# Attention scores and row maxima in four 32-row tiles of TensorE in place of two 64-row tiles

## The chip, the cores and the metric

The kernel runs on one core of a Trainium2 chip. The metric is the device time of one execution in microseconds (us), the median of several runs. The engines are named as in the profile: PE is TensorE (matmuls; PEld is its weight load, which overlaps them), DVE is VectorE, ACT is ScalarE, POOL is GpSimd and SP is the sync engine, which issues the DMAs (SPq is its queue). Matmul results go to PSUM, here used as eight banks of 128 partitions x 512 fp32 numbers. "L246" is line 246 of the kernel before.

## The reference

One transformer block without biases, on 2048 tokens of width 448, in fp32: layer norm, multi-query attention (16 heads of 28 dimensions that share one key and one value head, softmax over all 2048 keys, output projection, residual), then layer norm and a gated feed-forward of width 1792 with a residual.

```python
q = (ln(x) @ wq) in 16 heads of 28;  k = ln(x) @ wk;  v = ln(x) @ wv
p = softmax(q k^T * 28 ** -0.5);     h = x + concat(p v) @ wo
out = h + (silu(ln(h) @ w1) * (ln(h) @ w3)) @ w2
```

## The kernel before

**Numbers in two parts.** Matmuls in the format fp32r keep fewer bits than fp32, so most operands are split into a rounded part and a rest, both fp32r, and a product is the sum of rounded x rounded, rest x rounded and rounded x rest. For a wide product these are separate matmuls that add up in one PSUM bank (`mm_D`, L121, line 128 in the profile). The product of weights and values (`pv`, L296, line 300) is in plain fp32; the profile shows two matmul instructions for each of its calls.

**Scores.** Scores are made transposed: 128 keys on the partitions, 512 queries along the row. A head has 28 dimensions, so with four spare rows it takes 32 partitions; the four heads of a group stand below each other in the projection's output. In the kernel before, a score matmul is 64 rows deep: `KS` holds the rounded keys on rows 0-31 and their rests on rows 32-63 (and a copy of both on rows 64-127), and the queries of one head are laid out twice, on both halves of the same 64 rows. So two matmuls per head (`Head.mm`, L282, line 287), with the rounded queries and with their rests, make all four partial products. Head `j` of a group uses rows 0-63 if `j` is even and 64-127 if it is odd. `build_qs` (L206) splits the queries into `qst` (ACT and POOL) and lays them out by eight DMAs (line 223) in `QS`.

**Row maxima.** Softmax needs each query's largest score before the exponential. It is found ahead by separate matmuls, the units (`Unit`, L228, line 241): rounded queries as the weights, so 128 queries stand on the partitions and 512 keys along the row, and one VectorE `tensor_reduce` (line 246) takes the maximum into `MX`. When all 64 units of a block are done, `max_done` (L256) reduces and splits the maxima into `NEG`, `max_rows` (L265) transposes it on VectorE, and `max_out` (L270) puts it by four DMAs (line 274) into spare rows of `QS`, which meet ones in `KS`. So the score matmul itself subtracts the maximum, and `Head.exp` (L289, line 293) is one ScalarE exponential from a bank to `pt`.

**The loop.** A block `i` is 512 queries and four heads (16 blocks), a step is one block with 128 keys (16 per block, 256 steps). In each of the first 236 steps (L626) TensorE does the four heads' scores of step `s`, four units of step `s + AHEAD` (20 steps on), and `pv` of step `s - 1`. The order in a step is written out by hand and differs between even and odd steps: `pair` makes two heads beside each other, `beside` a head and units. What happens at certain steps only (building queries, maxima, dividing by the softmax sum in `o_norm` and `o_mul`, splitting weights, `wo_rows`) is filed by step with `at` and called by `run`. The last 20 steps (L670) have no units left. A start stage (L382 to L564) does layer norm and the projections `kv` and `q` with the first 80 units between them (`first`, `pairs`); a feed-forward stage follows the loop.

**Banks.** Seven banks serve everything but `po`, the sum of `pv`, which has the eighth. `bank` takes the one longest in the free list and `done` appends it; both act when the program is written, so the assignment is fixed, and on the chip a matmul into a bank waits for the bank's last reader. The program order of each engine is the order in which the code names the operations.

Of the kernel before, what the change touches and what calls it, by code (L numbers as in the profile page):

```python
# [35 lines left out]
def block_kernel(  # L36
# [25 lines left out]
    qs_pool = ctx.enter_context(tc.tile_pool(name="qs", bufs=3))  # L62
# [9 lines left out]
    KS = keep.tile([P, S], F32R, name="KS", tag="ks")  # L72
# [20 lines left out]
    def put_w2_ks():  # L93
        tl = keep.tile([P, S], F32, name="w2_ks", tag="ks")
        for k in range(4):
            W2[4 + k] = tl[:, T * k : T * k + D]
# [9 lines left out]
    free, used = list(range(7)), {}  # L106

    def bank(name="pb"):
# [97 lines left out]
    def build_qs(i, ps=None):  # L206
        t, g = divmod(i, NG)
        st = wk_pool.tile([P, 2, T], F32R, name="qst")
        if ps is None:
            q = QR[t][:, g]  # L210
            se.activation(st[:, 0], q, AF.Copy)  # L211
            ge.tensor_tensor(st[:, 1], q, f(st[:, 0]), op=ALU.subtract)  # L212
        else:
            se.activation(st[:, 0], ps, AF.Copy)
            ve.tensor_tensor(st[:, 1], ps, f(st[:, 0]), op=ALU.subtract)
# [12 lines left out]
    class Unit:  # L228

        def __init__(self, i, p, n, kt, jj):
            self.i, self.p, self.n, self.kt, self.jj = i, p, n, kt, jj

        def mm(self):
            i, n, kt, r = self.i, self.n, self.kt, rows(self.jj)
# [3 lines left out]
            pe.matmul(self.ps, QS[i][r, self.p, n * P : (n + 1) * P], KS[r, kt * T : (kt + 1) * T],  # L241
                      start=True, stop=True)

        def red(self):
            c = 8 * self.jj + 4 * self.p + self.n
            ve.tensor_reduce(MX[self.i][:, c, self.kt : self.kt + 1], self.ps, axis=AX.X, op=ALU.max)  # L246
            done(self.ps)

    def both(i, p, n, kt):
        us = [Unit(i, p, n, kt, jj) for jj in range(2)]  # L250
        for u in us:
            u.mm()
        for u in us:
            u.red()

    def max_done(i):  # L256

        nm, neg = wk_pool.tile([P, 16], F32, name="nm"), NEG[i % 2]
        ve.tensor_reduce(nm, MX[i], axis=AX.X, op=ALU.max, negate=True)
        hi, lo = [neg.rearrange("q (j k c) -> q j k c", j=2, k=2)[:, :, k] for k in range(2)]  # L260
        n2 = nm.rearrange("q (j c) -> q j c", j=2)
        ge.tensor_copy(hi, n2)
        ge.tensor_tensor(lo, n2, f(hi), op=ALU.subtract)
# [6 lines left out]
    def max_out(i):  # L270
        mr = f(MR.pop(i))
        to = f(QS[i][28::32, :2]).rearrange("m p (n a q) -> m (p n) a q", n=NQ, a=4)
        for a in range(4):
            sy.dma_start(to[:, :, a], mr[32 * a : 32 * a + 32])

    class Head:
# [5 lines left out]
        def mm(self, k):  # L282
            i, c, (p, jj) = self.i, self.c, divmod(self.j, 2)
            if k == 0:
                self.ps = bank()
            r = rows(jj)
            pe.matmul(self.ps, KS[r, c * P : (c + 1) * P], QS[i][r, 2 * k + p], start=(k == 0), stop=(k == 1))  # L287

        def exp(self):  # L289
            i, c, (p, jj) = self.i, self.c, divmod(self.j, 2)  # L290
            if (i, c, p) not in PT:
                PT[i, c, p] = pt_tile()
            se.activation(f(PT[i, c, p][:, jj]), self.ps, AF.Exp, bias=0.0, scale=SCALE)  # L293
            done(self.ps)

    def pv(i, c):  # L296
        if c == 0:
            PO[i] = ps_o.tile([P, T], F32, name="po")
        for j in range(4):
            pe.matmul(PO[i][32 * j : 32 * j + 32], VA[:, c], f(PT[i, c, j // 2][:, j % 2]),  # L300
                      start=(c == 0), stop=(c == NC - 1))
        if c == NC - 1:
            g = i % NG
            if i < NI - 2:
                se.activation(OT[:, g], PO.pop(i), AF.Copy)
# [48 lines left out]
    def split_w(k):  # L354
        ws = qs_pool.tile([P, 4, T], F32R, name="qs")
        wh, wl = [ws[:, 2 * b : 2 * b + 2].rearrange("p a (c m e) -> p (a c) m e", c=2, m=2) for b in range(2)]
        ve.tensor_copy(wh, W13[k])
        ge.tensor_tensor(wl, W13[k], f(wh), op=ALU.subtract)  # L358
        return wh, wl

    def split_w2(k):
        w2s = wk_pool.tile([P, 2, T], F32R, name="qst")
# [3 lines left out]

    def a_units(step):

        i, c = divmod(step, NC)
        if i >= NI:  # L370
            return None
        p, n = divmod(c // 2, NQ)
        us = [Unit(i, p, n, 2 * (c % 2) + k, jj) for jj in (1, 0) for k in range(2)]
        return us if step % 2 == 0 else [us[0], us[2], us[3], us[1]]

# [6 lines left out]
    with tc.tile_pool(name="start", bufs=1) as sp:  # L382
        wq_r = wo_r = OT[:, :, :D]
        WQ = [w.rearrange("p c (h r) -> p c h r", h=H) for w in OS]
        wkv_r = sp.tile([P, 4, 96], F32, name="wkv_r")
        WKV = [sp.tile([P, 4, 96], F32R, name=f"WKV{k}") for k in range(2)]
        ones = sp.tile([P, 1], F32, name="ones")
        ve.memset(wkv_r, 0.0)
        se.activation(ones, ident[:, 60:61], AF.Identity, bias=ident[:, 28:29], scale=-1.0)
# [3 lines left out]
        for m0, w in ((0, wk), (64, wv)):  # L393
# [5 lines left out]
        def copy_wk():  # L399
            ve.tensor_copy(wkv_r[:, :, 32 : 32 + DH], wkv_r[:, :, :DH])  # L400
# [32 lines left out]
        def kv(t, nb=0):  # L433
            cols = slice(t * T, (t + 1) * T)
            ps = bank()
            mm_D(ps[:96], WKV, XT[t], slice(0, 96), slice(0, T), lambda: pairs(nb))

            se.activation(KS[0:64, cols], ps[0:64], AF.Identity, bias=ones[0:64], scale=1.0)
            ve.tensor_tensor(KS[32:64, cols], ps[32:64], f(KS[32:64, cols]), op=ALU.subtract)
            vt = sp.tile([P, T], F32, name="vt", bufs=2)  # L440
            se.activation(vt[64:96], ps[64:96], AF.Copy)
            sy.dma_start(f(KS[64:128, cols]), f(KS[0:64, cols]))
# [3 lines left out]
        def va(t, vt):  # L446
            ps = bank()
            for n in range(NQ):
                pe.transpose(ps[:, 32 * n : 32 * n + 32], vt[64:96, n * P : (n + 1) * P], ident[64:96, 64:96])  # L449
# [14 lines left out]
        first = [(both, 0, *divmod(pn, NQ), kt) for kt in range(4) for pn in range(8)]  # L464
        first.append((max_done, 0))
        for c in range(AHEAD - NC):
            first += [(both, 1, *divmod(c // 2, NQ), 2 * (c % 2) + k) for k in range(2)]
# [150 lines left out]
    def pair(a, b):  # L618
        for k in range(2):
            a.mm(k)  # L620
            b.mm(k)
        a.exp()
        b.exp()

    prev, tail = None, False
    for s in range(LAST - AHEAD):  # L626
        i, c = divmod(s, NC)
        au = a_units(s + AHEAD)
        hs = [Head(i, c, j) for j in range(4)]

        def beside(h, us):
            for k in range(2):
                h.mm(k)
                us[k].mm()
            h.exp()

        def red(us):
            for u in us:
                u.red()

        pair(hs[0], hs[1])
        if c % 2 == 0:
            beside(hs[2], au[:2])
            run(s + 0.4)
            red(au[:2])
            run(s + 0.5)
            if prev is not None:
                pv(*prev)
            run(s + 0.7)
            beside(hs[3], au[2:])  # L650
            red(au[2:])
        else:
            pair(hs[3], hs[2])
            for u in au[:2]:
                u.mm()
            run(s + 0.4)
            red(au[:2])
            run(s + 0.5)
            pv(*prev)
            run(s + 0.7)  # L660
            for u in au[2:]:
                u.mm()
            red(au[2:])
        prev = (i, c)
        run(s)
# [3 lines left out]
    TAIL = LAST - AHEAD  # L669
    for s in range(TAIL, LAST):  # L670
        i, c = divmod(s, NC)
# [4 lines left out]
        hs = [Head(i, c, j) for j in range(4)]  # L676
        for k in range(2):
            hs[0].mm(k)
            hs[1].mm(k)
        if s == TAIL:  # L680
            pv(*prev)
# [3 lines left out]
        hs[0].exp()  # L685
        hs[1].exp()
        pair(hs[2], hs[3])
# [127 lines left out]
```

## Time and profile before

| | |
|---|---|
| median of 3 runs | 1219.92 us (1219.85 to 1220.7) |
| profiled execution, first to last instruction (its own time, in the span) | 1218.0 us |
| granted TensorE clock, mean | 1.000 |
| DMA traffic of the span | 47.34 MB, mean 39 GB/s |
| first and last exponential of the attention loop's heads | at 90 and 774 us |
| first and last reduce of a unit | at 31 and 735 us |

The page's first table gives each engine's busy time and its share of the span. A group's row reads: line, engine, operation, output<-inputs, shapes, count, then busy time, mean ns of one, idle time of the engine just before, and what ended most of it. A row of the timeline reads: start, length, engine, line, operation, count. A row of the windows reads: stretch, its length, busy time (count) of PE, PEld, DVE, ACT and POOL, granted clock, DMA share, GB/s.

### The profile page before, as it was taken

The numbers are of one execution on the slowest core, as the hardware profiler recorded it, in microseconds if no ns is written. First come the engines' busy times: TensorE is split into PE (matmuls) and PEld (weight loads), VectorE is DVE, ScalarE is ACT, GpSimd is POOL, SyncE is SP. The second block draws the span as 40 slices with busy tenths as digits, with TensorE's granted clock in tenths as the row PEclk, the third lists the DMA queues.
The fourth block names the chain that finished last, engine by engine and source line by source line (L and its number), as shares of the span: only waits on it lengthen the run. The fifth ranks groups of instructions, "written<-read, shape, count | busy, mean of one in ns | idle before, by whom it ended". The sixth has DMA issues, their size and how long they took to land.

```text
span 1218.0 us, 19886 instructions
## 1 busy us (share of the span) xinstructions
PE 1204.7 (99%) x7564; PEld 760.6 (62%) x7564; DVE 858.8 (71%) x1476; ACT 663.4 (54%) x1251; POOL 332.0 (27%) x281
## 2 busy tenths in 40 slices
PE   6999999999999999999999999999999999999998
PEld 5764444446444445444446444688888888888887
DVE  7999999998999998999998992164343334333333
ACT  4427887885888885888786789512111111111111
POOL 4320001101001110110122012254555555555552
PEclk9999999999999999999999999999999999999999
DMA  6120111211210221221121100133000000000000
GB/s 205 33 70 1 46 39 46 52 44 50 52 43 12 53 51 42 53 47 35 26 57 42 47 18 19 49 85 110 1 31 1 1 1 31 1 1 31 1 1 31
DMA packets 46526, 47.34 MB, mean 39 GB/s; under 512 B 14944, under 2 KB 33120, under 8 KB 46432
## 3 DMA queue, kind: packets, MB, share of 16 engines
q1 hardware_dynamic: 46432, 46.09, 14.4%
q8 instruction: 59, 0.97, 0.3%
q14 instruction: 35, 0.29, 0.1%
HBM read 20.37 MB, written 3.80 MB: 20 GB/s over the span
## 4 chain that ended last, share of the span: by engine, by line
PE 98%; DVE 1%; DMA 0%; SPq 0%; ACT 0%; issue 0%; POOL 0%; DVEq 0%
PE pa L128 27%; PE pb L287 26%; PE po L300 21%; PE pb L722 11%; PE pa L241 8%; PE pb L128 4%; PE pb L190 1%; DMA wkv_r<-in_A_wk_dram 0%; DVE st L156 0%; DVE xn L174 0%; DVE X L726 0%; SPq L378 0%; DVE mx L246 0%; DVE OS L411 0%; PE pb L449 0%
## 5 line engine op out<-in xcount | busy, mean ns | idle before, releaser
L246 DVE TENSOR_REDUCE mx<-pa 128x1 f32<-128x512 f32 x1024 | 637.0, 683 | 26.0 <-PE pa L241 3.1
L293 ACT ACTIVATE pt<-pb 128x512 f32<-128x512 f32 x996 | 517.8, 602 | 125.1 <-PE pb L287 96.2
L287 PE MATMUL pb<-qs,KS 64*128 64x512 f32 x2048 | 348.6, 399 | 0.0
L287 PEld LDWEIGHTS pb<-qs,KS 64*128 64x128 f32 x2048 | 227.7, 184 | 142.2 <-DVE mx L246 95.9
L241 PE MATMUL pa<-KS,qs 64*128 64x512 f32 x1024 | 283.2, 437 | 0.1
L300 PE MATMUL po<-pt,VA 128*32 128x512 f32 x1992 | 265.0, 604 | 0.0
L128 PE MATMUL pa<-xh,qs 128*128 128x512 f32 x896 | 235.2, 395 | 0.0
L241 PEld LDWEIGHTS pa<-KS,qs 64*128 64x128 f32 x1024 | 129.1, 184 | 129.6 <-DVE mx L246 103.2
L128 PEld LDWEIGHTS pa<-xh,qs 128*128 128x128 f32 x896 | 168.6, 188 | 37.8 <-issue 0.8
L710 DVE TENSOR_TENSOR pt<-pa,pt 128x512 f32<-128x512 f32 x56 | 38.7, 691 | 205.7 <-PE pa L128 205.7
L722 PE MATMUL pb<-qst,pt 128*128 128x448 f32 x672 | 147.8, 368 | 0.0
L708 ACT ACTIVATE pt<-pa 128x512 f32<-128x512 f32 x56 | 33.5, 599 | 193.9 <-PE pa L128 193.7
L722 PEld LDWEIGHTS pb<-qst,pt 128*128 128x128 f32 x672 | 125.2, 188 | 13.6 <-DVE pt L714 0.3
L713 ACT ACTIVATE pt<-pt 128x512 fp32r<-128x512 f32 x56 | 35.4, 633 | 157.5 <-DVE pt L710 157.5
L128 PE MATMUL pa<-xl,qs 128*128 128x512 f32 x336 | 96.3, 395 | 0.0
L300 PEld LDWEIGHTS po<-pt,VA 128*32 128x32 f32 x1992 | 40.1, 108 | 78.8 <-issue 74.5
L358 POOL TENSOR_TENSOR qs<-QR,qs 128x1024 fp32r<-128x1024 f32 x32 | 76.8, 2400 | 25.6 <-PE pa L128 16.2
L128 PEld LDWEIGHTS pa<-xl,qs 128*128 128x128 f32 x336 | 63.3, 188 | 14.6
L714 DVE TENSOR_TENSOR pt<-pt 128x512 fp32r<-128x512 f32 x56 | 44.7, 798 | 39.1 <-ACT pt L713 39.1
L329 POOL TENSOR_TENSOR OT<-OT,rb 128x512 f32<-128x512 f32 x15 | 19.3, 1289 | 190.6 <-DMA rb<-sd 166.0
L364 POOL TENSOR_TENSOR qst<-w_wo,qst 128x448 fp32r<-128x448 f32 x24 | 35.8, 1490 | 94.2 <-DVE qst L363 94.2
L212 POOL TENSOR_TENSOR qst<-QR,qst 128x512 fp32r<-128x512 f32 x15 | 19.3, 1285 | 145.4 <-ACT qst L211 145.4
(90 smaller groups left out, 656.7 us busy)
## 6 DMA issues: line engine op xcount, KB each, us to landing
qs<-qst SPq DMA_DIRECT2D x128, 128.0 KB
rb<-sd SPq DMA_DIRECT2D x64, 64.0 KB
QR<-OT SPq DMA_DIRECT2D x60, 56.0 KB
QR<-in_B_w_dram SPq DMA_DIRECT2D x16, 192.0 KB
X<-in_A_x_dram SPq DMA_DIRECT2D x3, 896.0 KB
out_dram<-X SPq DMA_DIRECT2D x3, 896.0 KB
w<-in_B_w_dram SPq DMA_DIRECT2D x8, 192.0 KB
w_wo<-in_B_w_dram SPq DMA_DIRECT2D x6, 224.0 KB
```

Source lines behind the costliest of these rows:

```text
L128: pe.matmul(ps, lhs[b][:, cb, lsl], rhs[a][:, ca, rsl], start=(k == 0), stop=(k == len(terms) - 1),)
L241: pe.matmul(self.ps, QS[i][r, self.p, n * P : (n + 1) * P], KS[r, kt * T : (kt + 1) * T], start=True, stop=True)
L246: ve.tensor_reduce(MX[self.i][:, c, self.kt : self.kt + 1], self.ps, axis=AX.X, op=ALU.max)
L287: pe.matmul(self.ps, KS[r, c * P : (c + 1) * P], QS[i][r, 2 * k + p], start=(k == 0), stop=(k == 1))
L293: se.activation(f(PT[i, c, p][:, jj]), self.ps, AF.Exp, bias=0.0, scale=SCALE)
L300: pe.matmul(PO[i][32 * j : 32 * j + 32], VA[:, c], f(PT[i, c, j // 2][:, j % 2]), start=(c == 0), stop=(c == NC - 1))
L358: ge.tensor_tensor(wl, W13[k], f(wh), op=ALU.subtract)
L364: ge.tensor_tensor(w2s[:, 1, :D], W2[k], f(w2s[:, 0, :D]), op=ALU.subtract)
L710: ve.tensor_tensor(sg, ps[1], sg, op=ALU.mult)
L713: se.activation(h[:, 0], sg, AF.Copy)
L714: ve.tensor_tensor(h[:, 1], sg, f(h[:, 0]), op=ALU.subtract)
L722: pe.matmul(Y[t][n][:, :D], hid[a][:, n * P : (n + 1) * P], w2s[:, b, :D], start=(k == 0 and m == 0), stop=(k == NF - 1 and m == 2))
```

## The change

A head's scores are made in a row tile of its own, 32 rows deep, four tiles side by side. The rounded keys (`KS[0]`) and their rests (`KS[1]`) become two tiles, each with four copies below each other, and the queries stay as the projection leaves them, four heads below each other, rounded part and rest in `QS[i][:, 0]` and `[:, 1]`. A head now takes three matmuls (rounded x rounded, key rest x rounded query, rounded key x query rest), and a unit uses one row tile. The eight DMAs of `build_qs` go; `max_out` issues eight DMAs of 16 rows instead of four of 32, for rounded maxima and rests separately (spare rows 28 and 29 of each tile). The order within two steps is the list `EVERY`: `h0` is the next of three matmuls for heads 0 and 1, `h1` for heads 2 and 3, `u3` a unit in row tile 3, and `pv` the product with the values; what is filed for a step is called around `pv`. `bank` picks the free bank that is due first by a running count, to which `on_pe` adds matmul times and `read_by` those of the readers. The ring `qs` has seven tiles of half the size; in the feed-forward stage a weight's two parts take two of them, and the parts of `w2` go to a tile in the place of `KS[1]`.

```diff
-    KS = keep.tile([P, S], F32R, name="KS", tag="ks")
+    KS = [keep.tile([P, S], F32R, name=f"KS{k}", tag=f"ks{k}") for k in range(2)]
...
     def bank(name="pb"):
-        k = free.pop(0)
+        k = min(free, key=lambda k: order[k])
+        free.remove(k)
+        clock["pe"] = max(clock["pe"], order[k])
...
-    def done(ps):
-        free.append(used.pop(id(ps))[1])
+    def done(ps, at=0.0):
+        k = used.pop(id(ps))[1]
+        order[k] = max(at, clock["pe"] + 0.5)
+        free.append(k)
...
-        QS[i] = qs_pool.tile([P, 4, T], F32R, name="qs")
-        for p in range(2):
-            for jj in range(2):
-                for b in range(2):
-                    r, j = 64 * jj + 32 * b, 2 * p + jj
-                    sy.dma_start(f(QS[i][r : r + 32, p::2]), f(st[32 * j : 32 * j + 32]))
-
-    def rows(jj):
-        return slice(64 * jj, 64 * jj + 64)
+    def rows(j):
+        return slice(32 * j, 32 * j + 32)
+
+    def on_pe(us):
+        clock["pe"] += us
+
+    def read_by(eng, every, last):
+        t = clock[eng] = max(clock["pe"] + 0.5, clock[eng])
+        clock[eng] = t + every
+        return t + last
...
-            done(self.ps)
+            done(self.ps, read_by("dve", 0.6, 0.7))
...
-        to = f(QS[i][28::32, :2]).rearrange("m p (n a q) -> m (p n) a q", n=NQ, a=4)
-        for a in range(4):
-            sy.dma_start(to[:, :, a], mr[32 * a : 32 * a + 32])
+        for k in range(2):
+            to = f(QS[i][28 + k :: 32, 0]).rearrange("j (n a q) -> j n a q", n=NQ, a=4)
+            for a in range(4):
+                r = 32 * a + 16 * k
+                sy.dma_start(to[:, :, a], mr[r : r + 16])
...
-            pe.matmul(self.ps, KS[r, c * P : (c + 1) * P], QS[i][r, 2 * k + p], start=(k == 0), stop=(k == 1))
+            pe.matmul(self.ps, KS[k % 2][r, c * P : (c + 1) * P], QS[i][r, k // 2], start=(k == 0), stop=(k == 2))
+            on_pe(0.057)
...
-            done(self.ps)
+            done(self.ps, read_by("act", 0.48, 0.66))
...
-            ve.tensor_tensor(KS[32:64, cols], ps[32:64], f(KS[32:64, cols]), op=ALU.subtract)
+            ve.scalar_tensor_tensor(KS[1][0:96, cols], ps[0:96], ones[0:96], f(KS[0][0:96, cols]),
+                                    op0=ALU.add, op1=ALU.subtract)
...
-            sy.dma_start(f(KS[64:128, cols]), f(KS[0:64, cols]))
+            for k in range(2):
+                sy.dma_start(f(KS[k][96:128, cols]), f(KS[k][0:32, cols]))
...
+    def scores(p):
+
+        s, k = divmod(left[p], 3)
+        if s == LAST:
+            return
+        left[p] += 1
         i, c = divmod(s, NC)
+        if k == 0:
+            heads[p] = [Head(i, c, 2 * p + jj) for jj in range(2)]
+        for h in heads[p]:
+            h.mm(k)
+        if k == 2:
+            for h in heads[p]:
+                h.exp()
+
+    def unit(j):
+
+        s = units[j] + AHEAD
+        if s < LAST:
+            units[j] += 1
+            i, c = divmod(s, NC)
+            u = Unit(i, j, *divmod(c, NQ))
+            u.mm()
+            u.red()
+
+    EVERY = "h0 u3 h1 u1 h1 h0 h1 u0 pv h1 u1 h0 h1 u2 u0 h1 h0 u3 h0 h0 u2 pv".split()
+
+    s = 0
+    while s < TAIL:
+        for x in EVERY:
+            if x != "pv":
+                (scores if x[0] == "h" else unit)(int(x[1]))
+                continue
             run(s + 0.4)
             run(s + 0.5)
+            if s > 0:
+                pv(*divmod(s - 1, NC))
             run(s + 0.7)
+            run(s)
+            s += 1
```

The last 20 steps call `scores` for both pairs in turn, with `pv` at the same places as before.

More of the change, by code (lines that the diff above doesn't have):

```diff
@@ L93, in put_w2_ks @@
     def put_w2_ks():
[L94 removed]
+        tl = keep.tile([P, S], F32, name="w2_ks", tag="ks0")
         for k in range(4):
@@ L359, in split_w @@
         return wh, wl
+    w2s_home = []
     def split_w2(k):
-        w2s = wk_pool.tile([P, 2, T], F32R, name="qst")
+        if k == 0 and not w2s_home:
+            w2s = qs_pool.tile([P, 2, T], F32R, name="qs")
+        else:
+            if not w2s_home:
+                w2s_home.append(keep.tile([P, 2, 2, T], F32R, name="w2s", tag="ks1"))
+            w2s = w2s_home[0][:, k % 2]
         ve.tensor_copy(w2s[:, 0, :D], W2[k])
@@ L684, in block_kernel @@
             pv(*divmod(s - 2, NC))
-        hs[0].exp()
-        hs[1].exp()
-        pair(hs[2], hs[3])
+        while left[0] < 3 * (s + 1) or left[1] < 3 * (s + 1):
+            for p in range(2):
+                if left[p] < 3 * (s + 1):
+                    scores(p)
         run(s + 0.4)
```

127 lines of the change are left out of this document (40 added, 87 removed).

## The prediction

> **What bounds the kernel now.** I read the page's busy table and groups first, then the windows by stage, then the timeline of a few steps inside the attention loop, because an average over the span hides what ends a step.
>
> ```profile
> span 1218.0 us, 19886 instructions
> PE 1204.7 (99%) x7564; PEld 760.6 (62%) x7564; DVE 858.8 (71%) x1476; ACT 663.4 (54%) x1251; POOL 332.0 (27%) x281
> L246 DVE TENSOR_REDUCE mx<-pa 128x1 f32<-128x512 f32 x1024 | 637.0, 683 | 26.0 <-PE pa L241 3.1
> L293 ACT ACTIVATE pt<-pb 128x512 f32<-128x512 f32 x996 | 517.8, 602 | 125.1 <-PE pb L287 96.2
> 300.00:400.00 100.00, 100.00 (x762) 48.61 (x760) 94.97 (x161) 79.59 (x154) 9.18 (x11) 1.00 0.17 40
> ```
>
> The last row is a window of the attention loop: TensorE 100 us of 100, VectorE 95, ScalarE 80, clock 1.00. Two engines are nearly full there, so a step may not shrink much however little TensorE has to do. The timeline of two steps says which of them ends it (start, length, engine, line, count):
>
> ```profile
> 399.41 1.07 PE L300 MATMUL po<-pt,VA 128*32 128x512 f32 x8
> 400.40 0.50 PE L241 MATMUL pa<-KS,qs 64*128 64x512 f32 x2
> 400.74 0.86 PE L287 MATMUL pb<-qs,KS 64*128 64x512 f32 x5
> ...
> 401.44 0.39 PE L287 MATMUL pb<-qs,KS 64*128 64x512 f32 x1
> ...
> 401.77 1.06 PE L300 MATMUL po<-pt,VA 128*32 128x512 f32 x8
> 402.76 0.50 PE L287 MATMUL pb<-qs,KS 64*128 64x512 f32 x1
> ...
> 403.10 1.31 PE L287 MATMUL pb<-qs,KS 64*128 64x512 f32 x9
> 403.53 2.58 ACT L293 ACTIVATE pt<-pb 128x512 f32<-128x512 f32 x5 [0.49 <-PE pb L287]
> 404.18 0.19 PEld L241 LDWEIGHTS pa<-KS,qs 64*128 64x128 f32 x2 [0.20 <-ACT pt L293]
> 404.25 0.43 PE L241 MATMUL pa<-KS,qs 64*128 64x512 f32 x2
> 404.61 1.07 PE L300 MATMUL po<-pt,VA 128*32 128x512 f32 x8
> ```
>
> The `pv` calls (L300) start 2.36 and 2.84 us apart: **5.20 us for two steps**. From a `pv`'s start to the next score matmul it is 0.99 us (401.77 to 402.76). Score matmuls run two at a time, on rows 0-63 and 64-127. The nine matmuls from 403.10 are one beside a unit's, then four pairs: (1.31 - 0.39)/4 = 0.23 us a pair, which I call a slot. The first slot behind a `pv` is 0.34 (400.40 to 400.74; 402.76 to 403.10), since its successor's weights aren't yet loaded, and from the last slot's start to `pv` it is 0.36 (404.25 to 404.61). The long half, seven slots, adds up: 0.99 + 0.34 + 5 x 0.23 + 0.36 = 2.84. The short half, five slots, likewise gives 2.36. No wait is left over: TensorE ends the step. VectorE's floor is close:
>
> ```profile
> 90.02 4.90 DVE L246 TENSOR_REDUCE mx<-pa 128x1 f32<-128x512 f32 x8
> 93.58 1.06 PE L300 MATMUL po<-pt,VA 128*32 128x512 f32 x8
> 94.58 0.50 PE L241 MATMUL pa<-KS,qs 64*128 64x512 f32 x2
> 95.11 1.29 DVE L246 TENSOR_REDUCE mx<-pa 128x1 f32<-128x512 f32 x2 [0.18 <-PE pa L241]
> 733.76 1.07 PE L300 MATMUL po<-pt,VA 128*32 128x512 f32 x8
> ```
>
> Queued reduces follow each other every (4.90 - 0.68)/7 = 0.60 us, and two steps have eight: 4.82 us. The loop, 236 steps or 118 pairs of steps, reaches from 93.58 to about 734. Even perfect cover by VectorE would bring only (5.20 - 4.82) x 118 = 45 us.
>
> **The change, part by part.** *Slots.* Head and unit matmuls become 32 rows deep: three per head instead of two, in four row tiles. Two steps have 32 instead of 24. No row shows four row tiles at once. A slot of four costs between 0.23 (as two do now) and 0.46 (two pairs in turn); I take 0.23, the nearest row, as the two halves of the array already don't hinder each other. Matmuls start in program order, so I number them by the row tile they need. `EVERY` ahead of its first `pv` is 0 1 3 2 | 3 1 2 | 3 0 1 2 | 3 0: four slots, 0.99 + 0.34 + 2 x 0.23 + 0.34 = **2.13** in place of 2.36. Behind it, 2 3 1 0 | 1 2 3 | 2 0 | 2 3 0 1 | 3 0 1 | 0 1 2: six slots, so 2.6 in place of 2.84 if nothing waits.
>
> *Banks.* Something does wait there. Latencies from the rows above: a matmul's reader starts 0.53 after it behind a `pv` (94.58 to 95.11), else 0.43 (403.10 to 403.53); exps follow each other every (2.58 - 0.60)/4 = 0.49; and a weight load starts 0.05 after the reader that frees its bank ends (403.53 + 0.60 to 404.18). Now count the seven banks when the second `h0` behind the first `pv` (the one that opens the next step's scores) is reached: two hold the `h1` pair, two the earlier `h0` pair, whose third matmuls have just run and whose exps come next, three hold `u1`, `u2`, `u0`. None is free. With the `pv`'s start as zero, `u1` runs at 0.99, its reduce 1.52 to 2.20, so the new `h0` pair starts at 2.25. `u3` behind it needs the bank of the second exp: 1.52 + 0.49 + 0.60 + 0.05 = 2.66. The second `h0` matmuls stand behind `u3` in TensorE's queue. Then a slot for the third ones and `u2`, and `pv` follows: 2.66 + 0.23 + 0.34 = **3.23** in place of 2.84. Choosing banks by the count of reader ends doesn't help: all seven are held.
>
> Two steps: 2.13 + 3.23 = 5.36 against 5.20, **+0.16 x 118 = +19 us**. Each of the latencies may be off by some 0.05, and two of them lie in the long half: 5.26 to 5.46, +7 to +31.
>
> *Row maxima.* `max_out` issues eight DMAs instead of four, and the first head matmul of a block needs them all.
>
> ```profile
> 124.81 1.07 PE L300 MATMUL po<-pt,VA 128*32 128x512 f32 x8
> 126.11 0.20 DVE L268 STREAM_TRANSPOSE mr<-neg 128x32 f32<-128x32 f32 x1
> 126.37 2.23 SPq L274 DMA_DIRECT2D qs<-mr  x4
> 131.34 0.85 PE L287 MATMUL pb<-qs,KS 64*128 64x512 f32 x5
> 129.20:129.40 0.20, 0.20 (x4) 0.19 (x2) 0.20 (x2) 0.20 (x1) 0.00 (x0) 1.00 0.14 20
> 129.40:130.00 0.60, 0.60 (x6) 0.19 (x2) 0.60 (x2) 0.60 (x3) 0.00 (x0) 1.00 0.00 0
> ```
>
> The transpose runs 1.30 after its `pv` starts, the first DMA is issued 0.26 later, and four take 2.23: one each 0.57. The last, issued at about 128.08, moves its bytes by 129.4 (DMA share 0.14, then 0.00): 1.3 us from issue. The block's first heads start at 131.34, 1.9 us in hand. After the change the transpose stands behind the same number of reduces, again some 1.3 behind that `pv`, and the eighth DMA lands at 1.56 + 7 x 0.57 + 1.3 = 6.85. The block's first `h0` is due one pair of steps and one `pv` later: 5.36 + 0.99 = 6.35. TensorE waits 0.5 us, 15 times: **+8** (0 if half as many rows issue faster, +15 if the transpose slips by a reduce). So the cover of today, 1.9 us, is used up.
>
> *The queries' own DMAs go.* `build_qs` issued eight per block:
>
> ```profile
> qs<-qst SPq DMA_DIRECT2D x128, 128.0 KB
> SPq L274 <- DVE mr L268: 225.6, 16, 38.5
> L305 ACT ACTIVATE OT<-po 128x512 f32<-128x512 f32 x14 | 8.6, 611 | 0.0
> 30.00:60.00 30.00, 30.00 (x154) 21.28 (x153) 28.93 (x54) 14.92 (x28) 10.41 (x14) 1.00 0.16 37
> 60.00:90.00 30.00, 30.00 (x139) 19.46 (x139) 27.53 (x48) 5.87 (x10) 7.04 (x11) 1.00 0.28 71
> 740.63 2.21 PE L287 MATMUL pb<-qs,KS 64*128 64x512 f32 x16
> ```
>
> The sync queue waits 225.6 us for the transposes alone, so it isn't late, and a block's queries are built long before use: nothing gained. *Block ends:* the copy of `po` (611 ns on ScalarE) now falls just ahead of the exps that free the banks: about 0.15 us each, +2 (0 to +9). *Start stage:* units may pair up four wide, saving up to 20 slots or 4.6 us, but VectorE idles only 1.07 + 2.47 us from 30 to 90, so at most 3.5; the doubled maxima DMAs, two more key copies and wider weights cost under 2: -1 (-3.5 to +2). *The last 20 steps* have no units: eight pairs of slots now (740.63, 2.21 us), and by the same numbering eight slots after; 0, with 1 us either way. *Feed-forward:* split tiles go through the ring of seven in pairs, three deep as before, and the `w2s` halves alternate as the two `qst` buffers did: 0. The three `wo_rows` blocks are the same.
>
> Sum: 19 + 8 + 2 - 1 = +28 us on a span of 1218.0: 1246. The median of the runs lies 1.9 above the span of the profiled execution; I keep that distance: **1248 us**.
>
> **The rivals.** *Faster: the banks come free in time and VectorE ends the step.* Two steps then take 4.82 plus about 0.1 for the small VectorE operations, -33 us; the maxima DMAs then are later still, 6.85 against 4.92 + 0.99, +14; in all 1200. It decides at one point: the total changes sign if `u3` gets its bank at 2.42 instead of 2.66 (then 2.42 + 0.57 = 2.99, the pair 5.12, -9 us, which the maxima give back). For it speaks that VectorE is already at 95%; against it the count of seven banks. *A slot of four row tiles is longer.* If it is a third of the way from 0.23 to 0.46, 0.30, the six plain slots on the path of two steps cost 0.07 more each: 5.78, +68 us, and the maxima then land almost in time (+2): about 1289. The rows can't exclude it, since they show two tiles at most. [...] *The change doesn't do what it says: only two tiles run at once.* 32 matmuls are 16 slots, 2 x (0.99 + 0.34 + 0.36) + 12 x 0.23 = 6.1 us, +106: 1325. The loads of both halves starting together (x2 in 0.19 at 404.18) speak against it. *The waits are a little shorter than I count*, both within their bounds: 1218 to 1231.
>
> **How the numbers follow.** Forecast, 1232 to 1264: 0.52. VectorE bound, around 1200 and up to 1217: 0.18. Longer slot, 1265 to 1300: 0.13. Two tiles at once: 0.05. Shorter waits: 0.12, of which 0.02 falls below and 0.05 within 0.2% (2.4 us, about what a measurement of this kernel can tell from no change). Faster 0.20, same 0.05, slower 0.75. The range 1205 to 1288 leaves out most of the VectorE case, the two-tile case and the top of the longer slot, 0.2 in all.
>
> **What would show it.** In the new timeline `pv` starts should alternate 2.1 and 3.2 us apart; four weight loads should start together; inside the long half the loads of `h0` and `u3` should wait for the reduce and the exp; VectorE should fall from 95 to about 92 of 100 us; the first head of a block should wait for the maxima's DMA by about 0.5 us. It would be wrong if the long half is under 3.0, if slots are over 0.25, or if a block's first head starts on time.

## The result and the profile after

The changed kernel takes **1317.58 us** (1315.32 to 1317.86, three runs) against 1219.92: a ratio of 1.0793 (95% interval 1.0774 to 1.0813), 98 us slower. The prediction had slower, but by 28 us, and its range ended at 1288. The profiled execution spans 1316.0 us against 1218.0, so the 98 us can be divided by stage from the two traces. The marks are the first `pv`, the last one with units beside it (235 later), and the last one of all (20 later):

| stage | before | after | difference | predicted |
|---|---|---|---|---|
| up to the first `pv` | 93.6 | 129.9 | +36.3 | -1 |
| first `pv` to the 236th | 640.2 | 695.1 | +54.9 | +29 |
| the last 20 steps | 40.3 | 47.2 | +6.9 | 0 |
| behind the last `pv` | 443.9 | 443.8 | -0.1 | 0 |

Nearly half of the loss lies in a stage that the prediction passed over in one sentence. The page of the kernel after, first its busy table, then the clock in 40 slices of 33 us, then two groups (L249 is the reduce and L296 the exponential):

```profile
span 1316.0 us, 21660 instructions
PE 1250.0 (95%) x8588; PEld 754.8 (57%) x8588; DVE 860.9 (65%) x1478; ACT 660.6 (50%) x1250; POOL 328.3 (25%) x281
...
PEclk9888999999999999999999999999999999999999
...
L249 DVE TENSOR_REDUCE mx<-pa 128x1 f32<-128x512 f32 x1024 | 636.1, 683 | 104.3 <-PE pa L244 53.6
L296 ACT ACTIVATE pt<-pb 128x512 f32<-128x512 f32 x996 | 514.1, 611 | 188.0 <-PE pa L244 122.7
```

Reduces and exponentials cost nearly what they did (683 and 611 ns; 683 and 602 before). What grew is the time in which their engines wait: 104.3 us ahead of the reduces (26.0 before), 188.0 ahead of the exponentials (125.1). The clock row has eights in slices 2 to 4, roughly 33 to 132 us.

**The start stage.** Windows of the kernel after; in each row the first busy time is TensorE's, the third VectorE's, and the granted clock stands third from the end:

```profile
30.00:60.00 30.00, 23.53 (x99) 15.57 (x97) 21.83 (x41) 11.05 (x20) 6.67 (x12) 0.89 0.03 6
60.00:90.00 30.00, 20.77 (x83) 13.13 (x83) 14.74 (x25) 6.75 (x12) 4.06 (x4) 0.79 0.09 20
90.00:120.00 30.00, 24.43 (x99) 15.22 (x96) 18.57 (x32) 3.58 (x6) 6.98 (x10) 0.87 0.06 19
...
400.00:500.00 100.00, 94.59 (x843) 40.50 (x845) 87.35 (x148) 73.55 (x144) 9.76 (x12) 1.00 0.05 12
```

Before, TensorE was busy for 30.00 of 30 us in the first two of these windows, with 154 and 139 matmuls; now it is busy for 23.53 and 20.77, with 99 and 83, and VectorE's 28.93 and 27.53 fell to 21.83 and 14.74. Neither engine is the bound, so something stands between them. The waits of TensorE's weight loads from 45 to 130 us (total, times, longest) and a stretch of the timeline name it. L134 is the projections' matmul, L244 a unit's, L465 ScalarE's copy of a finished query projection out of its bank, L444 its copy of the values:

```profile
PEld pb L134 <- ACT QR L465: 6.8, 6, 1.3
...
PEld pb L134 <- ACT vt L444: 3.9, 1, 3.9
```

```profile
48.17 1.29 PE L134 MATMUL pb<-xh,OS 128*128 128x512 f32 x5
50.15 0.96 PE L134 MATMUL pb<-xh,OS 128*128 128x512 f32 x3 [0.69 <-ACT QR L465]
...
52.40 1.43 PE L134 MATMUL pb<-xh,OS 128*128 128x512 f32 x5
54.51 0.96 PE L134 MATMUL pb<-xh,WKV 128*128 128x512 f32 x3 [0.69 <-ACT QR L465]
...
56.53 1.42 PE L134 MATMUL pb<-xh,WKV 128*128 128x512 f32 x5
60.45 0.79 PE L244 MATMUL pa<-KS,qs 32*128 32x512 f32 x4 [2.50 <-ACT vt L444]
```

A projection ends, TensorE stands still while ScalarE copies the result out, and only then does the next projection (or, in the last row, a unit) start. It waits for a copy of the very bank that it has just filled, although seven banks are there. Followed through `bank` and `done` in the order of the program, 15 of the stage's 20 projections hand their bank straight to the next taker, a projection, a unit or a transpose; in the kernel before none does. The reason is in the count by which `bank` now chooses. `Unit.mm`, `Head.mm` and `pv` move the count's TensorE time on by `on_pe`; `mm_D`, which makes the projections, doesn't. A unit adds 0.057 to that time and 0.6 to VectorE's, so a unit's bank is noted as due when VectorE's long queue reaches it, while a projection's bank, returned with no reader's time, is noted as due half a microsecond after a time that its own matmuls have not moved. It looks like the earliest of all, and the next projection takes it. Behind some of the standstills the granted clock falls as well:

```profile
58.00:60.00 2.00, 0.00 (x0) 0.00 (x0) 2.00 (x4) 0.87 (x2) 0.00 (x0) 1.00 0.06 14
60.00:62.00 2.00, 1.55 (x6) 1.01 (x7) 0.94 (x3) 0.40 (x1) 0.24 (x1) 0.63 0.22 51
62.00:64.00 2.00, 2.00 (x6) 1.52 (x6) 1.75 (x3) 0.00 (x0) 0.00 (x0) 0.52 0.00 0
```

Those are windows of 2 us around the standstill of 2.50 us. TensorE does nothing from 58 to 60, and the granted clock falls to 0.63 and 0.52 behind it. Not every standstill goes with a fall: five of 0.69 us between 105 and 123 us left the clock at 1.00, while five of the six spells at half clock (0.50 granted) up to the first `pv` begin during or within 2 us behind a standstill of 1.6 to 3.45 us (83.60 to 87.05 is the longest; the spell from 125.4 has none before it, and its cause stays open). Over 30 to 120 us the means of 0.89, 0.79 and 0.87 amount to some 27 us at half clock (2 x 30 x (0.11 + 0.21 + 0.13)). From 25 us to the first `pv` TensorE stands still for 22.5 us (0.1 before) and has half clock for about 32; eight matmuls of `pv` take 1.94 us there (at 129.90) and 1.06 at full clock (at 136.51), so the latter is worth up to 16 us, an estimate, and since some of the standing still lies in it, the two account for about the 36.3.

**The loop.** Two steps in the middle, the timeline of the kernel after (L289 is a head's matmul, L303 `pv`, L277 the maxima's DMAs):

```profile
399.99 1.06 PE L303 MATMUL po<-pt,VA 128*32 128x512 f32 x8
...
400.99 0.50 PE L289 MATMUL pb<-qs,KS 32*128 32x512 f32 x2
...
400.99 0.49 PE L244 MATMUL pa<-KS,qs 32*128 32x512 f32 x1
...
401.00 0.50 PE L289 MATMUL pb<-qs,KS 32*128 32x512 f32 x1
...
401.43 4.98 SPq L277 DMA_DIRECT2D qs<-mr  x8
...
402.12 1.07 PE L303 MATMUL po<-pt,VA 128*32 128x512 f32 x8
...
403.12 0.49 PE L244 MATMUL pa<-KS,qs 32*128 32x512 f32 x1
...
403.72 3.08 DVE L249 TENSOR_REDUCE mx<-pa 128x1 f32<-128x512 f32 x5 [0.24 <-PE pb L289]
403.75 3.04 ACT L296 ACTIVATE pt<-pb 128x512 f32<-128x512 f32 x6 [0.55 <-PE pb L289]
...
404.46 0.18 PEld L289 LDWEIGHTS pb<-qs,KS 32*128 32x128 f32 x2 [0.59 <-DVE mx L249]
...
404.89 0.18 PEld L244 LDWEIGHTS pa<-KS,qs 32*128 32x128 f32 x1 [0.24 <-ACT pt L296]
...
404.89 0.50 PE L289 MATMUL pb<-qs,KS 32*128 32x512 f32 x2
...
405.23 0.40 PE L289 MATMUL pb<-qs,KS 32*128 32x512 f32 x2
...
405.56 1.06 PE L303 MATMUL po<-pt,VA 128*32 128x512 f32 x8
...
407.55 0.50 PE L289 MATMUL pb<-qs,KS 32*128 32x512 f32 x2 [0.92 <-DMA qs<-mr]
```

`pv` starts are 2.13 and 3.44 apart (399.99, 402.12, 405.56). In the long half two loads wait, first for the reduce (0.59, until 404.46), then for the second exponential (0.24, until 404.89), as the count of seven banks had it. At a block's end the first head stands until 407.55 for the eighth DMA. Over the whole loop this wait comes to

```profile
PE pb L289 <- DMA qs<-mr: 9.4, 10, 1.3
```

9.4 us in the ten ends of blocks where the trace names it. The arithmetic of the loop closes: 118 x (5.57 - 5.20) = 43.7, and eleven steps at ends of blocks are 0.6 to 1.4 longer than 2.13, together 10.8; of 54.9 that leaves 0.4.

**The last 20 steps**, two steps of the kernel after, TensorE and then ScalarE:

```profile
849.69 1.07 PE L303 MATMUL po<-pt,VA 128*32 128x512 f32 x8
...
854.41 1.92 PE L303 MATMUL po<-pt,VA 128*32 128x512 f32 x16
```

```profile
852.13 2.06 ACT L296 ACTIVATE pt<-pb 128x512 f32<-128x512 f32 x4 [0.69 <-PE pb L289]
...
856.85 1.58 ACT L296 ACTIVATE pt<-pb 128x512 f32<-128x512 f32 x3 [0.69 <-PE pb L289]
```

Two steps take 4.72 us (849.69 to 854.41) where they took 3.99 (7.98 for four, 746.75 to 754.73). Eight exponentials at 0.49 are 3.92, so ScalarE ended these steps before and worked without a stop. Now it stands 0.69 us once in two steps: of the first pair's matmuls the code puts two ahead of the two `pv`s, and a head now has three, so no exponential can start beside the `pv`s until the third has run behind them.

### The profile page after: what moved, and what is told of

It is laid out like the page before. It is cut to its first block, busy times and chain, and to the rows that moved or that the text cites. A ratio compares the mean times of both kernels' runs of the same rounds, so it can differ in the third digit from the quotient of the medians.

```text
span 1316.0 us, 21660 instructions
## 1 busy us (share of the span) xinstructions
PE 1250.0 (95%) x8588; PEld 754.8 (57%) x8588; DVE 860.9 (65%) x1478; ACT 660.6 (50%) x1250; POOL 328.3 (25%) x281
## 4 chain that ended last, share of the span: by engine, by line
PE 85%; DVE 8%; SPq 2%; DMA 1%; ACT 1%; issue 1%; POOL 0%; DVEq 0%
PE pa L134 25%; PE pb L289 20%; PE po L303 18%; PE pb L720 10%; PE pa L244 7%; DVE mx L249 6%; PE pb L134 4%; SPq L277 2%; DMA qs<-mr 1%; PE pb L196 1%; ACT QR L465 1%; ACT xh L197 0%; DVE xn L180 0%; DMA wkv_r<-in_A_wk_dram 0%; ACT pt L296 0%
## 5 line engine op out<-in xcount | busy, mean ns | idle before, releaser
L249 DVE TENSOR_REDUCE mx<-pa 128x1 f32<-128x512 f32 x1024 | 636.1, 683 | 104.3 <-PE pa L244 53.6
L296 ACT ACTIVATE pt<-pb 128x512 f32<-128x512 f32 x996 | 514.1, 611 | 188.0 <-PE pa L244 122.7
L289 PE MATMUL pb<-qs,KS 32*128 32x512 f32 x3072 | 451.4, 439 | 29.4 <-DVE mx L249 18.5
L289 PEld LDWEIGHTS pb<-qs,KS 32*128 32x128 f32 x3072 | 237.9, 183 | 294.9 <-DVE mx L249 165.1
L244 PE MATMUL pa<-KS,qs 32*128 32x512 f32 x1024 | 325.2, 470 | 7.4 <-ACT vt L444 4.1
L303 PE MATMUL po<-pt,VA 128*32 128x512 f32 x1992 | 266.4, 606 | 0.0
L134 PE MATMUL pa<-xh,qs 128*128 128x512 f32 x896 | 235.5, 395 | 0.0
L134 PEld LDWEIGHTS pa<-xh,qs 128*128 128x128 f32 x896 | 168.5, 188 | 37.6 <-issue 0.8
L244 PEld LDWEIGHTS pa<-KS,qs 32*128 32x128 f32 x1024 | 155.7, 185 | 50.8 <-ACT pt L296 28.6
L720 PE MATMUL pb<-w2s,pt 128*128 128x448 f32 x660 | 144.1, 367 | 0.0
L720 PEld LDWEIGHTS pb<-w2s,pt 128*128 128x128 f32 x660 | 123.1, 188 | 12.4
L134 PE MATMUL pa<-xl,qs 128*128 128x512 f32 x336 | 96.4, 395 | 0.0
L303 PEld LDWEIGHTS po<-pt,VA 128*32 128x32 f32 x1992 | 40.2, 108 | 88.2 <-issue 81.8
L263 POOL CAST neg<-nm 128x16 fp32r<-128x16 f32 x16 | 3.1, 197 | 291.8 <-DVE nm L262 291.8
L134 PEld LDWEIGHTS pa<-xl,qs 128*128 128x128 f32 x336 | 63.2, 188 | 14.9
L217 POOL TENSOR_TENSOR qs<-QR,qs 128x512 fp32r<-128x512 f32 x15 | 19.2, 1279 | 173.2 <-ACT qs L216 173.1
L375 POOL TENSOR_TENSOR w2s<-w_wo,w2s 128x448 fp32r<-128x448 f32 x24 | 34.4, 1432 | 95.0 <-DVE w2s L374 76.8
```

Source lines behind the costliest of these rows:

```text
L134: pe.matmul(ps, lhs[b][:, cb, lsl], rhs[a][:, ca, rsl], start=(k == 0), stop=(k == len(terms) - 1),)
L244: pe.matmul(self.ps, QS[i][r, 0, n * P : (n + 1) * P], KS[0][r, kt * T : (kt + 1) * T], start=True, stop=True)
L249: ve.tensor_reduce(MX[self.i][:, 4 * self.j + self.n, self.kt : self.kt + 1], self.ps, axis=AX.X, op=ALU.max)
L289: pe.matmul(self.ps, KS[k % 2][r, c * P : (c + 1) * P], QS[i][r, k // 2], start=(k == 0), stop=(k == 2))
L375: ge.tensor_tensor(w2s[:, 1, :D], W2[k], f(w2s[:, 0, :D]), op=ALU.subtract)
L720: pe.matmul(Y[t][n][:, :D], hid[a][:, n * P : (n + 1) * P], w2s[:, b, :D], start=(k == 0 and m == 0), stop=(k == NF - 1 and m == 2))
```

## The experiments

**Theory:** three separate causes: the bank choice is blind to the projections (start), the loop has too few banks for the new order (long half), and the maxima's DMAs come late (ends of blocks). **Rivals:** for the start, the doubled DMAs, the wider key weights or the units in 32 rows; for the loop, longer slots, the bank choice itself, or VectorE. Where a kernel builds on one that lacks the count's lines, line numbers are one lower (L302 is `pv`).

**1. The change without the counted choice of banks.**

```diff
-        k = min(free, key=lambda k: order[k])
-        free.remove(k)
-        clock["pe"] = max(clock["pe"], order[k])
+        k = free.pop(0)
+        clock["pe"] = max(clock["pe"], order[k])
```

> Only the choice of a bank goes back to the free list's order. Theory (banks): the start stage lost its 36 us because the count is not told of the projections' matmuls, so a projection takes back the bank that was just freed and waits for its reader; the first pv comes at about 94 us again and the clock stays at 1.00, the attention loop keeps 2.13 and 3.44 us between pv starts, in all about 1282 us. Rival (layout): the start lost its time to the new key and query layout and its DMAs; the first pv stays near 130 us, in all about 1316 us.

1285.87 us, 1.0540 (1.0523 to 1.0558) of before, 4 us above the expectation. The first `pv` starts at 96.57 instead of 129.9, and the windows are nearly full again:

```profile
30.00:60.00 30.00, 29.78 (x156) 21.42 (x155) 28.95 (x55) 15.37 (x29) 10.77 (x16) 1.00 0.04 10
60.00:90.00 30.00, 29.14 (x138) 18.89 (x136) 28.09 (x50) 5.88 (x10) 7.04 (x11) 1.00 0.13 36
90.00:120.00 30.00, 28.35 (x218) 12.92 (x218) 23.58 (x38) 18.81 (x37) 0.00 (x0) 0.83 0.01 1
```

So 33.3 of the start's 36.3 us are the choice of banks. The other 3.0 show in this trace as well, ahead of the first head:

```profile
84.93 4.68 SPq L276 DMA_DIRECT2D qs<-mr  x8
91.00 0.79 PE L288 MATMUL pb<-qs,KS 32*128 32x512 f32 x2 [1.73 <-DVE mx L248]
```

The reduce that the row names ended at 90.46; the last of the eight DMAs of block 0's maxima is recorded as landed at 90.66, and TensorE's queue waits for that signal until 90.9. Before, four DMAs had landed at 88.9, ahead of the first head at 89.83. Behind the 1.73 us the clock is at half from 90.5 to 100.8, so the loop's first two steps are late too (3.87 and 3.57 us). Otherwise the loop's halves stay at 2.12 and 3.43: there the choice makes no difference, as was predicted.

**2. The kernel before, with the counted choice alone.** All lines of the count, with 0.114 us for a 64-row matmul, and nothing else of the change.

```diff
-        k = free.pop(0)
+        k = min(free, key=lambda k: order[k])
+        free.remove(k)
+        clock["pe"] = max(clock["pe"], order[k])
...
+            on_pe(0.114)
...
-            done(self.ps)
+            done(self.ps, read_by("dve", 0.6, 0.7))
```

> The kernel before with only the counted choice of banks. Theory (banks): its start stage loses 25 to 36 us, its loop keeps 2.36 and 2.84 us since TensorE and not a bank ends its steps there; about 1250 us. Rival (layout): the count costs nothing by itself, about 1220 us.

1246.17 us, 1.0210 (1.0195 to 1.0225). The first `pv` moves from 93.58 to 119.99, +26.4, and the loop stays at 639.8 us:

```profile
60.00:90.00 30.00, 23.92 (x94) 15.59 (x92) 15.38 (x26) 7.22 (x13) 3.83 (x3) 0.77 0.28 71
```

The mean granted clock falls here too, to 0.77, without one 32-row matmul. The cause of the start's loss is independent of the tiles; only its size differs (26.4 against 33.3).

**3. The change with the count told of the projections.** This asks whether it is the blindness of the count, and not the idea of counting.

```diff
 def mm_D(...):
...
+            clock["pe"] += 0.23
```

> The changed kernel with the count told of the projections' matmuls too, 0.23 us each. Theory (the count is blind to them): the first pv comes at 94 to 99 us, in all about 1284 us. Rival (choosing by a count is bad in the start stage however it is kept): the first pv stays above 110 us, 1297 us or more.

1295.41 us (one run). The first `pv` comes at 104.95: 25 of the 33 us are back, between theory and rival. The blindness is most of it. The 8 us that remain against the simple order were not taken apart, but five of the 20 projections still hand their bank straight on, and units still wait 4.0 us in total for the copies of the values: the copies out of the banks and the transposes still aren't counted.

**4. and 5. One bank fewer, in both kernels** (the change with the simple choice, and the kernel before).

```diff
-    free, used = list(range(7)), {}
+    free, used = list(range(6)), {}
```

> The changed kernel with the free list's order and six banks in place of seven, the matmuls unchanged. Theory (banks): counted as for seven, the halves take 2.8 and 4.0 us, 6.8 for two steps, so the loop is 140 to 150 us longer than with seven. Rival (slots or readers' speed end the step, not banks): the halves stay within 0.3 us of 2.13 and 3.44.

> The kernel before with six banks in place of seven. Theory (banks): seven are just enough for it, with six it waits too; 6.0 us for two steps, 0.8 more, less than the 1.2 more of the changed kernel. Rival: two matmuls per head leave banks to spare, 5.2 to 5.4 us.

1430.49 and 1327.78 us (one run each). `pv` rows of the change with six banks, then of the kernel before with six:

```profile
420.06 1.06 PE L302 MATMUL po<-pt,VA 128*32 128x512 f32 x8
...
422.82 1.06 PE L302 MATMUL po<-pt,VA 128*32 128x512 f32 x8
...
426.86 1.07 PE L302 MATMUL po<-pt,VA 128*32 128x512 f32 x8
```

```profile
422.66 1.06 PE L300 MATMUL po<-pt,VA 128*32 128x512 f32 x8
...
428.69 1.06 PE L300 MATMUL po<-pt,VA 128*32 128x512 f32 x8
```

Two steps take 6.80 instead of 5.57 in the one, 6.03 instead of 5.20 in the other, as expected. (The first kernel's loop is 134 us longer, not 140 to 150: with slower steps the late ends of blocks are gone.) A bank is worth more to the four-tile order (1.23 us in two steps) than to the old one (0.83), but the old one answers too, so this alone doesn't show that seven are too few; the next experiment does. (The eighth bank belongs to `po`, so seven to eight wasn't tried.)

**6. The same matmuls in another order.** Each pair of heads does its three matmuls closer together, so that it holds its banks for a shorter time.

```diff
-    EVERY = "h0 u3 h1 u1 h1 h0 h1 u0 pv h1 u1 h0 h1 u2 u0 h1 h0 u3 h0 h0 u2 pv".split()
+    EVERY = "h0 u3 h0 h1 h0 h1 u0 u1 h1 pv h1 u1 h1 h1 u0 h0 u2 h0 h0 u3 u2 pv".split()
```

> The changed kernel with another order of the same 32 matmuls of two steps, in which each pair of heads does its three matmuls close together, so that it holds its banks for a shorter time. Theory (banks): the loads of the long half wait less for a reduce or an exp; pv starts 2.1 and 3.1 us apart, two steps 5.2 instead of 5.57, 118 times 0.37 = 44 us less, about 1274 us. Rival (slots): four row tiles side by side, or three matmuls per head, are what takes the time; the same matmuls in another order take 5.5 or more, 1310 us or more.

1296.65 us, 1.0627 (1.0611 to 1.0642). Half right. The `pv` rows are 2.12 and 3.12 apart, 5.24 for two steps as expected, so the order in which banks are opened and given back was what the long half waited for:

```profile
404.52 1.07 PE L303 MATMUL po<-pt,VA 128*32 128x512 f32 x8
...
406.64 1.06 PE L303 MATMUL po<-pt,VA 128*32 128x512 f32 x8
...
409.76 1.07 PE L303 MATMUL po<-pt,VA 128*32 128x512 f32 x8
```

But 118 x 0.32 = 38 us were due and 21 came. The same wait as before, over this kernel's loop:

```profile
PE pb L289 <- DMA qs<-mr: 15.5, 10, 1.9
```

15.5 instead of 9.4 us: a faster loop reaches the block's first head sooner, and the DMAs, which take as long as ever (4.10 us from the first issue to the eighth in most blocks of both), make it wait. The eleven steps at ends of blocks are now 3.4 to 4.6 instead of 2.13, together 19.9 us over it where they were 10.8. The steps behind them lose 6.6 us (0.7 before): the copy of `po` is no longer hidden there, and behind four of the eleven standstills the clock is at half for 3.4 us.

**7. The maxima sent one `pv` earlier** in the changed kernel.

```diff
-        at(NC * i - 2.3, max_rows, i)
-        at(NC * i - 2.3, max_out, i)
+        at(NC * i - 4 + 0.7, max_rows, i)
+        at(NC * i - 4 + 0.7, max_out, i)
```

> The changed kernel with the maxima's transpose and DMAs one pv earlier. Theory (eight DMAs on one queue land late): the gaps of 0.6 to 1.4 us at the ends of blocks go, 11 us, for about 0.5 us of VectorE waiting per block, so 1305 to 1312 us. Rival (the copy of po on ScalarE makes the gap): the gaps stay, 1317 us or more.

1314.79 us, 1.0777 (1.0761 to 1.0793): a gain of 3 us, not of 5 to 12, and the single runs of the two kernels overlap. In the trace the loop is 2.6 us shorter. The wait for the DMAs is gone from the list, and another is there (VectorE's transpose for GpSimd's split of the maxima, once per block):

```profile
DVE mr L269 <- POOL neg L264: 9.0, 15, 0.7
```

VectorE stands 0.6 us in front of the transpose, the reduces behind it are late, the banks that they free too, and one step per block takes 3.94 instead of 3.44. The wait was moved, not removed. It takes both ends: `max_done` earlier as well.

**8. All edits together**: simple choice, new order, `max_done` a step earlier, maxima as in 7 (the expectations of experiment 9 say one and a half steps of both; it is one), and in the last 20 steps the third matmul of the first pair ahead of the `pv`s.

```diff
-        at(NC * i - 3.5, max_done, i)
+        at(NC * i - 5 + 0.5, max_done, i)
...
-        for k in range(2):
+        for k in range(3):
```

> Four row tiles with every loss mended that the runs so far have shown: banks in the free list's order, the order of the run before with each pair's matmuls close together, the maxima's reduction one pv earlier and their transpose and DMAs one pv earlier, and in the last 20 steps the third matmul of the first pair ahead of pv. Theory (banks): pv starts 2.12 and 3.13 us apart, 5.25 for two steps, no gaps at the blocks' ends, the last steps about 4.4 us a pair of steps; 1220 plus 3 (start), 6 (loop) and 4 (last steps), about 1233 us. Rival (something of the four tiles is not found yet): 1245 us or more.

1249.51 us, 1.0242 (1.0225 to 1.0259), missing its expectation by 16 us and in the range of its rival; experiment 9 decides between them. (In its last steps a `pt` tile is overwritten before it is used, so part of the last two blocks isn't computed.) Start (95.2) and loop (651.2 us, no late block) came as expected; the last 20 steps took 57.8 instead of 47.2, since exponentials named ahead of a `pv` take the `pt` tile that it still has to read, and the `pv` then waits for them (1.97 us at 753.90 and at 772.02). The last edit was wrong in itself.

**9. and 10. The same without the last edit, and with it done rightly**: the third matmul ahead of the `pv`s, its exponentials named behind them.

```diff
-        for k in range(2):
+        held = []
+        for k in range(3):
             if left[0] < 3 * (s + 1):
-                scores(0)
+                scores(0, held)
...
+        for h in held:
+            h.exp()
```

> The changed kernel with the simple bank order, the list EVERY of the earlier experiment on order, and the row maxima sent earlier (max_done one and a half steps, max_rows and max_out about one and a half steps), but the last 20 steps as the change has them. The separate costs should add up: start about +2 (first pv near 95), loop about +11 over the kernel before (pv starts 2.13 and 3.12 apart, no longer steps at the ends of blocks but one of about 3.45 for the copy of po), last 20 steps about +7 (0.88 and 3.85 apart). Sum 1220 + 20 = 1240, 1237 to 1243. Rival: the last steps were not made worse by the third matmul alone in the earlier run of all edits, but by banks that the simple order hands out late; then they stay above 50 us and the run takes 1246 or more.

> As the run beside it, but in the last 20 steps the third score matmul of the first pair of heads stands ahead of the two pvs and its exponentials are named behind them, so that they take no pt tile that pv still reads. If the last 20 steps are longer because ScalarE has nothing to do during the two pvs, two steps should take about 4.4 instead of 4.73 and the run about 3 us less than its neighbour (1236 to 1238). If instead the row of seven banks holds them, nothing moves (within 1 us). In either case four row tiles stay slower than the 1220 of the kernel before.

1241.50 us, 1.0165 (1.0148 to 1.0182), and 1239.51 us, 1.0153 (1.0138 to 1.0168). In the first the parts add up: start +3.0, loop +12.3, last steps +8.5, sum 23.8 of a span 23.7 longer. The loop's 12.3 can be read further: 118 x (5.25 - 5.20) = 6; fourteen steps at ends of blocks of 3.45 instead of 3.12, in which the copy of `po` (0.63 us on ScalarE) stands ahead of the exponentials, 4.5; and the first two steps at half clock, as in experiment 1, 2.6; some single steps are 0.8 shorter. In the second run two of the last steps take 4.46:

```profile
777.71 1.92 PE L302 MATMUL po<-pt,VA 128*32 128x512 f32 x16
...
782.17 0.62 PE L302 MATMUL po<-xh,VA 128*32 128x512 f32 x2
```

and ScalarE stands 0.43 us in them instead of 0.69:

```profile
780.62 3.05 ACT L295 ACTIVATE pt<-pb 128x512 f32<-128x512 f32 x6 [0.43 <-PE pb L288]
```

So the cause given for the last 20 steps holds, for 0.26 of the 0.73; why ScalarE still stands for the 0.43 wasn't settled. The total is 2.0 us under its neighbour, not 3, and missed the expected 1236 to 1238; single runs of the two overlap, so the rows carry this reading and not the totals. With every fault mended that was found, except the late first head of the start, four row tiles are still 1.5% slower than before: some 79 of the 98 us lay in how the change was carried out, 19 are left (1239.51 against 1220.42 beside it).

## Why the prediction was wrong, point by point

**The step that failed is the start stage**, "-1 (-3.5 to +2)". Measured: +36.3, of which 33.3 go with the choice of banks (experiment 1), which is no term of that sum, and 3.0 with what the prediction had priced there (the doubled maxima DMAs above all, at "under 2" with the key copies and wider weights). Its sentence "Choosing banks by the count of reader ends doesn't help: all seven are held" was right of the loop (3.44 with the count, 3.43 without) and was never asked of the stage where matmuls exist that the count doesn't see. The prediction knew from its window rows that both engines were full from 30 to 90 us. In such a stage a stall has little cover, so an edit to the order of banks could not be taken as free there. Without this loss the changed kernel takes 1285.87 us, just inside the range, though with a loop that lost 54.9 instead of 29.

**Slots: right.** Four row tiles share a slot of 0.23; the short half is 2.13, as counted (0.99 + 0.34 + 2 x 0.23 + 0.34), and in the trace after four matmuls start from 400.99 to 401.00. Both rivals that rested on slots, the longer slot (1289) and two tiles at once (1325), fall, although the time came out near them: a total that fits a rival doesn't confirm it; rows can. The 0.30 us that the longer-slot rival took for a slot of four is shown by no run; the trace has 0.23 (two slots from 401.33 to 401.79).

**Banks: right in mechanism, too small.** The long half was counted as 3.23 and is 3.44; the pair costs +0.37 instead of +0.16, 43.7 us instead of 19. Two terms were short. Readers start 0.60 to 0.63 behind a matmul (403.12 to 403.72 and 403.75; over the loop 0.56 to 0.60 for waiting reduces and 0.62 to 0.63 for waiting exponentials) where 0.53 was taken from before, which shifts the second exponential's end and with it `u3`, from 2.66 counted to 2.77 (404.89 - 402.12). And the slot behind the load that waited is 0.34 long (404.89 to 405.23), not 0.23: as behind a `pv`, the next weights had not been loaded beside the slot ahead (their loads start at 405.00 and 405.06). 2.77 + 0.34 + 0.33 = 3.44. Why readers start 0.07 to 0.10 later here isn't shown: no run varied the number of matmuls that end together alone.

**Maxima: right in mechanism, a little small.** The block's first head starts 7.56 after the transpose's `pv` (399.99 to 407.55) where 6.85 was counted. DMAs are issued 0.57 apart as counted, but for the first gaps: 4.46 from the first issue to the eighth here and 4.10 in most blocks, where 7 x 0.57 = 3.99 was counted. And the eighth is recorded as landed 1.57 after its issue (405.89 to 407.46), not 1.3. The wait against the due time (405.56 + 0.99 = 6.56 after it) is 1.0 instead of 0.5, and all ends of blocks cost 10.8 instead of 8, eleven of them where 15 were counted.

**Block ends by the copy of `po`**, +2 (0 to +9): right in mechanism, but hidden. In the changed kernel two steps behind ends of blocks take 3.77 instead of 3.44, and the others don't show it. Where the wait for the DMAs is gone (experiment 9) it is 0.33 in each of fourteen blocks, 4.5 us. **The last 20 steps**, 0: measured +6.9. Pairs of slots were counted there, but ScalarE was what ended those steps, and the right question was which matmul its first exponential waits for. **Feed-forward**, 0: -0.1, right.

**The rivals.** VectorE as the bound (1200) was refuted in the loop: its busy time fell to 87.35 of 100 us. Its point of decision, `u3` at 2.42, wasn't reached: 2.77. That the waits might be shorter was the wrong side; they were longer. No rival had a fault in the start stage, so no chance was kept for it, and the range ended 30 us short.

## What to carry to other kernels

When a change replaces a rule that the whole program uses (which bank, which buffer, which queue), ask it in every stage, first in those where no engine has time to spare, and look for work that the rule's bookkeeping doesn't see. Four row tiles fitted four matmuls into the 0.23 us that took two before, but opened as many accumulators, for longer: count held banks at the tightest point before counting slots, and take the latency of a matmul's reader from a place where as many matmuls end together (here 0.56 to 0.63 us, not 0.53). And a loop made faster meets its fixed-time transfers sooner: experiment 6 gave back almost half of what it had won, most of it at the ends of blocks.

## What the runs showed of the hardware

Behind single standstills of TensorE of 1.6 to 3.45 us the granted clock was at half (0.50) for 3.4 to 10.2 us: with the simple order one of 1.73 us went with 10.2, the window 90:120 shows 0.83, and the step behind the first `pv` took 3.87 us. Length alone didn't decide. In the loop of experiment 6 eleven standstills of 1.2 to 1.9 us came at ends of blocks, and four of them (1.25, 1.32, 1.56 and 1.92 us) went with 3.4 us at half clock, while ones of 1.82 and 1.74 didn't; those of 0.69 between 105 and 123 us in the changed kernel didn't either. Four matmuls of 32 rows x 512 columns ran at the pace of two of 64 rows, 0.23 us. Behind four that ended together the waiting readers of the loop started 0.56 to 0.63 us after them, where a row of the kernel before has 0.53 (94.58 to 95.11). Small DMAs of 2 KB and of 4 KB were issued alike, 0.57 us apart behind the first gaps, so eight in place of four took about twice as long to issue (from the first issue to the last 1.85 us before, 4.10 after, in most blocks). And a weight load that waited for a bank held up the loads behind it: those of the next heads started at 404.89 together with `u3`'s, and the slot after it was 0.34 instead of 0.23.
